# A transformer layer on one core: the head's values by single row tiles, the tail's second half turned earlier, kept pairs copied at once

## The chip, the cores and the metric

The kernel runs on one core of a Trainium2 chip. The metric is the device time of one execution in microseconds. The engines are named as the profile names them: PE does the matmuls (PEld is its loading of the stationary operand), ACT the activation functions, DVE the elementwise work and the reductions, POOL small extra work, and SP issues the transfers. Every engine has its own queue and works through it in order; engines wait for one another by semaphores.

## The reference, cut to what matters

One layer of a transformer on 2048 rows of width 1024, in bf16. The attention has 32 heads of width 32, the FFN 3584 units:

```python
def _A_ref(x, wqkv, wo):                       # H = 32, Dh = 32
    q, k, v = split_heads(x @ wqkv)
    p = softmax(einsum("bhqd,bhkd->bhqk", q, k) * Dh ** -0.5)
    return merge_heads(einsum("bhqk,bhkd->bhqd", p, v)) @ wo

def _B_ref(x, w1, b1, w2, b2):
    return gelu_tanh(x @ w1 + b1) @ w2 + b2

h = x + _A_ref(layernorm(x), wqkv, wo)
out = h + _B_ref(layernorm(h), w1, b1, w2, b2)
```

## The kernel before, in words

The 2048 rows are 16 row tiles of 128, or four chunks of 512. The 32 heads are eight groups of four. A planner in Python (`Plan`) writes out every engine's instruction list: each operation has a cost in ns, the planner keeps the time at which each engine is free and each buffer ready, and places operations by these times. The hardware then runs the fixed lists, with the waits that the planner derived from buffers read and written.

**The head** (lines 757 to 968) is placed by a list scheduler. A job is a step of one engine: `S` the statistics of a row tile (two `bn_stats` and a `bn_aggr` on DVE, L482 and L484), `R` and `I` the root and the reciprocal for a pair of tiles (POOL L495 to L497, DVE L498), `N` the normalising (DVE L801 or ACT L804), `T` the turning by PE (eight transposes, L512) and `C` its copy into `xnT` (ACT or DVE, L829); row tiles 6 to 13 are turned by DMA (L733). `K` and `Q` are matmuls for the first key group and the first four query groups (L843), `KE`, `QE` their copies (DVE L849, ACT L851), `KS`, `QS` the squares (ACT L859 or DVE). `Kn1` to `Kn4` and `Qn1` to `Qn4` reduce the squares to the largest norm (L870, L876, L877, L881, L886). `V` makes the values of two row tiles for the first two head groups (16 matmuls into one PSUM bank, L898), and `VE` copies them (L910).

A job may start when the jobs it depends on are placed. For each job the scheduler takes the engine on which it ends first, with a surcharge `LEAN` (ns) for DVE; on each engine it takes, among the jobs that can start within `WAIT` ns of the first, the one with the smallest priority number, and of the engines' picks it places the one that starts first. `SP` holds the shifts of the priorities: with the numbers before, `N` of tile tt has tt + 1, `C` tt - 2, `KE` and the like -6 on their own number, and `VE` 100 - 90. The loop ends when both norms are there; values not made by then are made later, by `proj_v` in the list `v_left`.

From the norms comes a bound on the scores, and from it a bias per group (`bias_of`, L708 to L714) that keeps the exponential in range, and a flag: where the bound is small the exponential runs without a bias. The first exponential waits for the first group's bias and flag.

**The middle** runs the attention, 1024 exponentials on ACT (L1215, 128x1024 each), 16 for an item of one head group and 256 rows. PE makes scores (L1206) and weighted values (L1291), and in between it is given steps of a "fill" (L530, the helper `wide`): first the values left over, then the other groups' keys, values and queries, then for each chunk the output projection, the norm and the FFN of the chunk before. The fill has PSUM bank 7 for itself. Near the end the fill makes "early slices" for the last chunk: pairs of FFN units for its first 256 rows, with weights `w_e`, as long as there is time and at most ten pairs (`FC // 2 - AHEAD`). Their sums with the bias (L1786) are kept in `gT_t` until the tail, and the gelu is applied there, since the function table then changes from exponential to gelu.

**The tail** (`tail`) projects the last 256 rows, normalises them (`last_norm(1)`), and runs four more pairs for the first half of the chunk (`for hf in range(2)`, hf 0, `AHEAD` is 4), then turns the second half (`last_turn(1)`: 16 transposes L512, two DVE copies L1439), then the same four pairs for the second half, then the other pairs, then the second FFN matmul and the output. `gelu` (L1827) reads each pair from PSUM, `held_gelu` (L1847) applies the function to four kept units at a time.

Of the kernel before, what the change touches and what calls it, by code (L numbers as in the profile page):

```python
# [13 lines left out]
P = 128  # L14
# [221 lines left out]
def build_kernel(nc, A_x, A_wqkv, A_wo, B_w1, B_b1, B_w2, B_b2, out):  # L236
# [120 lines left out]
    lnf, B_lnf0 = sb("lnf", [P, NLN, 4, 2], dt.float32, nbufs(1))  # L357
    half, (B_half,) = sb("half", [P, 4], dt.float32)
    lnd, B_lnd = sb("lnd", [P, NLN, 4], dt.bfloat16, nbufs(NLN * 2))
    lnb, B_lnb = sb("lnb", [P, 8, 2], dt.float32, nbufs(8))  # L360
# [4 lines left out]
    pool(lambda g: g.memset(lnf[:], 0.0), writes=B_lnf0 + B_lnm + B_lnv)  # L365
    pool(lambda g: g.memset(half[:], 0.5), writes=[B_half])
    warm, (B_warm,) = sb("warm", [P, 1], dt.float32)
    rcp, B_rcp = sb("rcp", [P, 2, 8], dt.float32, nbufs(2))
# [336 lines left out]
    def bias_of(g, tc):  # L705
        i = tc * 2 + g // 4
        b = biasm[:, g, tc:tc + 1]
        dve(lambda v: v.tensor_tensor(b, qmax[:, i, g % 4:g % 4 + 1], kmax[:, g:g + 1], ALU.add),  # L708
            reads=[B_qmax[i], B_kmax[g]], writes=[B_bias[g][tc]])
# [4 lines left out]
        dve(lambda v: v.tensor_scalar(b, b, -0.505 * SCALE, None, ALU.mult), reads=[B_bias[g][tc]], writes=[B_bias[g][tc]])  # L714

# [175 lines left out]
    def vals_job(p):  # L891
        tt = 2 * p

        def emit(eng, bank):
            for u in range(2):
                tc, o = (tt + u) // 4, ((tt + u) % 4) * P
                for dc in range(DC):
                    pe(lambda p, u=u, tc=tc, o=o, dc=dc: p.matmul(ps[:, bank, u * 256:(u + 1) * 256], xnT[tc][:, dc, o:o + P], wv[:, dc, 0:256],  # L898
                                                                  start=(dc == 0), stop=(dc == DC - 1)),
                       reads=B_wv[0:1] + [B_xnTf[tt + u]], writes=[B_ps[bank]] if dc in (0, DC - 1) else [], inc=(dc == DC - 1), cost=mm(256))  # L900
        job(("V", p), {E.PE: 1790}, [("C", tt), ("C", tt + 1)], 100 + p, B_wv[0:1] + B_xnTf[tt:tt + 2], [], emit, opens=True)

        def emit2(eng, bank):
            o_ap = V[:, tt:tt + 2, 0:256]
            i_ap = ps[:, bank, :].rearrange("p (u c) -> p u c", u=2)
            B_o = [B_V[tt][0], B_V[tt + 1][0]]
            if eng == E.DVE:
                dve(lambda v: v.tensor_copy(o_ap, i_ap), reads=[B_ps[bank]], writes=B_o, cost=700)
            else:
                act(lambda a: a.activation(o_ap, i_ap, ACT.Copy), reads=[B_ps[bank]], writes=B_o, cost=510)  # L910
# [22 lines left out]
    while ("kn", 0) not in marks or ("qn", 0, 0) not in marks:  # L933
        cand = {}
        for j in jobs.values():
# [23 lines left out]
        j.emit(e_, bank)  # L959
        if j.bank:  # L960
            held.discard(bank)
# [798 lines left out]
    def early_slices():  # L1760
# [7 lines left out]
        while early["n"] < FC // 2 - AHEAD and not early["stop"]:  # L1768
# [7 lines left out]
            for u in range(2):  # L1776
                for dc in range(DC):
                    B = B_w1_[k * 4 + dc // 2:k * 4 + dc // 2 + 1]
                    if dc % 4 == 0 and coming:
# [3 lines left out]
                         [B_ps[bank]] if dc in (0, DC - 1) else [], dc == DC - 1, quad)  # L1783
            for u in range(2):
                fc = 2 * bk + u
                dve(lambda v, fc=fc, u=u: v.tensor_tensor(gT[:, fc, 0:256], ps[:, bank, u * 256:u * 256 + 256], b1f[:, fc:fc + 1].to_broadcast([P, 256]), ALU.add),  # L1786
                    reads=[B_ps[bank], Bf_b1f], writes=[B_gT[2 * fc]], cost=420)
        while coming:
            coming.popleft()()

    def tail():
# [318 lines left out]
```

## Time and profile before

| | |
|---|---|
| median of 3 runs | 1130.21 us (1129.67 to 1131.08) |
| profiled execution | 1129.03 us |
| its span | 1127.2 us |
| first exponential | 48.45 us |
| end of the last exponential, start of the tail | 1030.65 us |
| busy over the span | PE 95%, ACT 92%, DVE 60%, weight loads 58% |

The span is the time from the first to the last instruction that the profile holds; the execution's own time has 1.8 us more around it. Times in the rows are microseconds from the start of the span. In the timeline a row is start, length, engine, line, operation, result<-operands, shapes, count; what stands in brackets is the idle time of that engine just before it and what ended it. In the list of waits a row is the waiting instruction, what it waited for, microseconds in total, number of times, the longest. In groups of one line the three numbers behind the count are the shortest, the median and the longest duration in ns.

### The profile page before, as it was taken

Reading aid. Unit: us, or ns where it says so; the run is one execution under the profiler, and the core shown is the slowest. Engines: PE = TensorE matmul, PEld = TensorE weight load, DVE = VectorE, ACT = ScalarE, POOL = GpSimd, SP = SyncE. Lnnn points to the kernel's source line nnn. Section 1 sums busy time; section 2 is a strip of 40 time slices with the busy share of each in tenths; the row PEclk is TensorE's granted clock in tenths of the full one; section 3 lists DMA queues with packets and bytes.
Section 4 is the critical chain, followed back from the end, with each engine's and each line's share of the span. In section 5 each row is a group of like instructions: output and inputs, shape, how many; then the busy total and the mean of one; then the engine's idle time right before and its main releaser. Section 6 shows DMA issues by size and latency. Waiting matters only on the chain.

```text
span 1127.2 us, 55337 instructions
## 1 busy us (share of the span) xinstructions
PE 1074.9 (95%) x25677; PEld 653.2 (58%) x25682; DVE 681.2 (60%) x1241; ACT 1032.3 (92%) x1149; POOL 21.7 (2%) x67
## 2 busy tenths in 40 slices
PE   6999999998999999999999999999999999999999
PEld 3556465644444446765444457775444676675888
DVE  7565656555767786555678785455577856556021
ACT  6799999999999999999999999999999999996510
POOL 2100000000000000000000000000000000000000
PEclk9999999999999999999999999999999999999999
DMA  9701000023422343424513432402224531427763
GB/s 273 130 22 41 22 3 12 14 63 77 93 68 77 107 114 97 126 77 97 86 59 88 127 115 79 124 23 74 77 80 124 149 83 49 117 83 197 183 160 90
DMA packets 212792, 103.72 MB, mean 92 GB/s; under 512 B 62032, under 2 KB 209488, under 8 KB 212560
## 3 DMA queue, kind: packets, MB, share of 16 engines
q1 hardware_dynamic: 212560, 100.18, 34.0%
q8 instruction: 201, 3.29, 1.2%
q14 instruction: 31, 0.25, 0.1%
HBM read 91.23 MB, written 4.19 MB: 85 GB/s over the span
## 4 chain that ended last, share of the span: by engine, by line
ACT 43%; PE 42%; issue 9%; DVE 5%; DMA 0%; SPq 0%; ACTq 0%; DVEq 0%
ACT PT L1215 40%; PE ps L530 18%; PE ps L525 8%; PE ps L1291 7%; PE ps L1206 6%; ACT tm L1610 2%; PE ps L843 1%; PE ps L898 1%; DVE Rg L1304 1%; DVE Rg L1302 1%; DVE QT L1306 1%; PE ps L637 0%; DVE gT L1594 0%; DVE lnst L482 0%; DVE rcp L1303 0%
## 5 line engine op out<-in xcount | busy, mean ns | idle before, releaser
L1215 ACT ACTIVATE PT<-ps 128x1024 bf16<-128x1024 f32 x1024 | 951.9, 1163 | 4.6 <-DVE biasm L714 2.6
L1240 DVE TENSOR_TENSOR FS<-PT 128x1024 bf16<-128x1024 bf16 x256 | 174.9, 688 | 140.7 <-ACT PT L1215 118.4
L1291 PE MATMUL ps<-PT,V 128*32 128x256 bf16 x4096 | 223.3, 274 | 9.2 <-DVE QT L1306 4.7
L1206 PE MATMUL ps<-QT,KT 32*128 32x256 bf16 x4096 | 203.9, 273 | 19.3 <-ACT PT L1215 13.9
L530 PE MATMUL ps<-hnT,w 128*32 128x512 bf16 (+1 forms) x2880 | 174.0, 367 | 4.3 <-DVE gT L1594 2.7
L530 PE MATMUL ps<-w,gT 128*32 128x256 bf16 x5376 | 173.2, 273 | 0.8 <-issue 0.6
L1206 PEld LDWEIGHTS ps<-QT,KT 32*128 32x128 bf16 x4096 | 60.9, 92 | 170.5 <-ACT PT L1215 148.4
L530 PEld LDWEIGHTS ps<-w,gT 128*32 128x32 bf16 x5376 | 141.0, 97 | 10.8 <-issue 4.6
L1291 PEld LDWEIGHTS ps<-PT,V 128*32 128x32 bf16 x4096 | 105.2, 96 | 55.1 <-issue 13.8
L1291 PE MATMUL ps<-PT,ones 128*32 128x256 bf16 x2048 | 129.2, 273 | 0.0
L530 PEld LDWEIGHTS ps<-hnT,w 128*32 128x32 bf16 x2880 | 65.7, 96 | 71.2 <-issue 27.1
L1594 DVE TENSOR_TENSOR gT<-ps,b1f 128x512 bf16<-128x512 f32 x84 | 57.9, 690 | 51.3 <-PE ps L530 50.9
L1291 PE MATMUL ps<-FS,ones 128*32 128x256 bf16 x1024 | 73.4, 277 | 0.0
L1291 PEld LDWEIGHTS ps<-PT,ones 128*32 128x32 bf16 x2048 | 55.0, 97 | 10.7
L530 PE MATMUL ps<-xnTe,wk 128*32 128x512 bf16 x832 | 56.5, 381 | 0.5 <-DVE KT L585 0.5
L1611 DVE SCALAR_TENSOR_TENSOR gT<-tm,gT 128x1024 bf16<-128x1024 bf16 x42 | 51.1, 1219 | 3.4 <-ACT tm L1610 2.9
L1609 DVE SCALAR_TENSOR_TENSOR tm<-tm,gT 128x1024 bf16<-128x1024 bf16 x42 | 51.3, 1221 | 0.8
L1610 ACT ACTIVATE tm<-tm 128x1024 bf16<-128x1024 bf16 x42 | 50.9, 1215 | 0.0
L525 PE MATMUL ps<-w,gT_t 128*128 128x256 bf16 x448 | 49.1, 273 | 0.0
L525 PEld LDWEIGHTS ps<-w,gT_t 128*128 128x128 bf16 x448 | 43.8, 98 | 5.1
L1291 PEld LDWEIGHTS ps<-FS,ones 128*32 128x32 bf16 x1024 | 26.9, 95 | 24.2 <-issue 20.9
L1827 ACT ACTIVATE gT_t<-ps,b1f 128x256 bf16<-128x256 f32 (+1 forms) x36 | 15.6, 482 | 24.7 <-PE ps L525 24.7
(142 smaller groups left out, 893.9 us busy)
## 6 DMA issues: line engine op xcount, KB each, us to landing
w<-in_B_w_dram SPq DMA_DIRECT2D x45, 512.0 KB, 3.9
w<-in_B_w_dram SPq DMA_DIRECT2D x168, 128.0 KB, 3.7
w_t<-in_B_w_dram SPq DMA_DIRECT2D x12, 512.0 KB, 6.1
w_e<-in_B_w_dram SPq DMA_DIRECT2D x44, 128.0 KB, 2.4
xr<-in_A_x_dram SPq DMA_DIRECT2D x16, 256.0 KB, 6.9
wk<-in_A_wqkv_dram SPq DMA_DIRECT2D x16, 256.0 KB, 3.2
wq<-in_A_wqkv_dram SPq DMA_DIRECT2D x16, 256.0 KB, 5.2
w<-in_B_w_dram SPq DMA_DIRECT2D x14, 256.0 KB, 6.1
```

The costliest lines, as they stand in the source:

```text
L525: pe(lambda p: p.matmul(ps[:, bank, lo:lo + n], lhsT, rhs, start=start, stop=stop), reads=reads, writes=writes, inc=inc, cost=mm(n))
L530: pe(lambda p, r=r: p.matmul(ps[32 * r:32 * r + 32, bank, lo:lo + n], lhsT[:, 32 * r:32 * r + 32], rhs, start=start, stop=stop, tile_posit ...
L843: pe(lambda p, dc=dc: p.matmul(ps[:, bank, :], w_of(dc), xnT[tc][:, dc, :], start=(dc == 0), stop=(dc == DC - 1)), reads=B_w + xn_of(tc), ...
L1206: pe(lambda p, k=k, kt=kt, r=r, b=b: p.matmul(ps[:, b, k * 256:(k + 1) * 256], KT[32 * r:32 * r + 32, g, kt * P:(kt + 1) * P], QT[32 * r:3 ...
L1215: act(lambda a, safe, i=i, b=b: a.activation(PT[:, o_, 2 * i:2 * i + 2, :], ps[:, b:b + 2, :], ACT.Exp, bias=0.0 if safe else biasm[:, g, ...
L1240: dve(lambda v: v.tensor_tensor(FS[:, f_, :, :], PT[:, o_, :, 0:256], PT[:, o_, :, 256:512], ALU.add), reads=B_PT[o_], writes=[B_FS[f_]], ...
L1291: pe(lambda p, d=d, r=r, lhsT=lhsT, rhs=rhs, n=n: p.matmul(ps[32 * r:32 * r + 32, OD, d * 256:(d + 1) * 256], lhsT, rhs, start=(start and ...
L1594: dve(lambda v: v.tensor_tensor(gT_[0][:, fcs[0]:fcs[0] + k, lo:lo + n], ps[:, bank, :].rearrange("p (u c) -> p u c", u=k), b1f[:, fcs[0]: ...
L1609: (E.DVE, lambda v: v.scalar_tensor_tensor(t_, t_, GB, x_, ALU.add, ALU.mult), [Bt] + Bx, [Bt], 1220),
L1610: (E.Activation, lambda a: a.activation(t_, t_, ACT.Tanh, scale=GK), [Bt], [Bt], 946),
L1611: (E.DVE, lambda v: v.scalar_tensor_tensor(x_, t_, 1.0, x_, ALU.add, ALU.mult), [Bt] + Bx, Bx, 1220)])
L1827: act(lambda a: a.activation(gT[:, fc, lo:lo + n], ps[:, bank, o:o + n], ACT.Gelu_apprx_tanh, bias=b1f[:, fc:fc + 1], scale=1.0), reads=[B ...
```

## The change

Head: `bias_of` takes the sum of the norms and the maximum with the bound in one operation (`safe_c` holds the bound per partition), and the shift and the scale in another, three operations in place of four. `WAIT` goes from 500 to 50 ns, the surcharges `LEAN` and the priority shifts `SP` get other numbers, and the surcharges hold only while statistics are still to be placed, except for `VE` and `QS`. A pair of values is made by two jobs, `V` for the first row tile and `W` for the second (priority 99), in the same bank. Values left over are copied by DVE in place of ACT.

Tail: the second half is turned before the fourth pair of the first half instead of behind it. Early slices: one addition for the two units of a pair, in place of two.

```diff
+    safe_c, (B_safe,) = sb("safe_c", [P, 1], dt.float32)
...
+    pool(lambda g: g.memset(safe_c[:], SAFE / (0.505 * SCALE)), writes=[B_safe])
...
-        dve(lambda v: v.tensor_tensor(b, qmax[:, i, g % 4:g % 4 + 1], kmax[:, g:g + 1], ALU.add),
-            reads=[B_qmax[i], B_kmax[g]], writes=[B_bias[g][tc]])
+        dve(lambda v: v.tensor_scalar(b, qmax[:, i, g % 4:g % 4 + 1], kmax[:, g:g + 1], safe_c[:, 0:1], ALU.add, ALU.max),
+            reads=[B_qmax[i], B_kmax[g], B_safe], writes=[B_bias[g][tc]])
...
-        dve(shift_op(b, b), reads=[B_bias[g][tc]], writes=[B_bias[g][tc]])
-        dve(lambda v: v.tensor_scalar(b, b, -0.505 * SCALE, None, ALU.mult), reads=[B_bias[g][tc]], writes=[B_bias[g][tc]])
+        dve(lambda v: v.tensor_scalar(b, b, -SAFE / (0.505 * SCALE), -0.505 * SCALE, ALU.add, ALU.mult), reads=[B_bias[g][tc]], writes=[B_bias[g][tc]])
...
-    WAIT = 500.0
-    LEAN = {"N": 600.0, "C": 1000.0, "M": 600.0, "KE": 300.0, "QE": 300.0, "QS": 5000.0, "VE": 5000.0}
+    WAIT = 50.0
+    LEAN = {'N': 1000, 'C': 600, 'M': 1000, 'KE': 300, 'KS': 0, 'QE': 5000, 'QS': 300, 'VE': 600}
...
-        def emit(eng, bank):
-            for u in range(2):
-                tc, o = (tt + u) // 4, ((tt + u) % 4) * P
+        def half(u):
+            tc, o = (tt + u) // 4, ((tt + u) % 4) * P
+
+            def emit(eng, bank):
                 for dc in range(DC):
...
+            return emit
+        job(("V", p), {E.PE: 895}, [("C", tt), ("C", tt + 1)], 100 + p, B_wv[0:1] + B_xnTf[tt:tt + 2], [], half(0), opens=True)
+        job(("W", p), {E.PE: 895}, [("V", p)], 99, B_wv[0:1] + B_xnTf[tt + 1:tt + 2], [], half(1), bank=("V", p))
...
-        job(("VE", p), {E.DVE: 700, E.Activation: 510}, [("V", p)], 100 + SP[5], [], [], emit2, bank=("V", p))
-
-    SP = (1.0, 0.0, 1.0, -2.0, -6.0, -90.0)
+        job(("VE", p), {E.DVE: 700, E.Activation: 510}, [("W", p)], 100 + SP[5], [], [], emit2, bank=("V", p))
+
+    SP = (1.0, 0.0, 2, 1, 3, -90)
...
-            end, st, e_ = min(o, key=lambda q: q[0] + (LEAN.get(j.name[0], 0.0) if q[2] == E.DVE else 0.0))
+            lean = LEAN.get(j.name[0], 0.0) if any(("S", tt) in jobs for tt in range(NT)) or j.name[0] in ("VE", "QS") else 0.0
+            end, st, e_ = min(o, key=lambda q: q[0] + (lean if q[2] == E.DVE else 0.0))
...
-        if j.bank:
+        if j.bank and j.name[0] != "W":
             held.discard(bank)
...
         if ("V", p) not in jobs and ("VE", p) in jobs:
+            if ("W", p) in jobs:
+                jobs[("W", p)].emit(E.PE, bank_of[("V", p)])
             jobs[("VE", p)].emit(E.Activation, bank_of[("V", p)])
-    v_left = [proj_v(2 * p, 0, "act") for p in range(NT // 2) if ("V", p) in jobs]
+    v_left = [proj_v(2 * p, 0) for p in range(NT // 2) if ("V", p) in jobs]
...
-            for u in range(2):
-                fc = 2 * bk + u
-                dve(lambda v, fc=fc, u=u: v.tensor_tensor(gT[:, fc, 0:256], ps[:, bank, u * 256:u * 256 + 256], b1f[:, fc:fc + 1].to_broadcast([P, 256]), ALU.add),
-                    reads=[B_ps[bank], Bf_b1f], writes=[B_gT[2 * fc]], cost=420)
+            fc = 2 * bk
+            dve(lambda v, fc=fc: v.tensor_tensor(gT[:, fc:fc + 2, 0:256], ps[:, bank, :].rearrange("p (u c) -> p u c", u=2),
+                                                 b1f[:, fc:fc + 2].unsqueeze(2).to_broadcast([P, 2, 256]), ALU.add),
+                reads=[B_ps[bank], Bf_b1f], writes=[B_gT[2 * fc], B_gT[2 * fc + 2]], cost=690)
...
             for bk in range(n, n + AHEAD):
+                if hf == 0 and bk == n + AHEAD - 1:
+                    yield from last_turn(1)
                 bank = fbanks.next()
...
-            if hf == 0:
-                yield from last_turn(1)
```

More of the change, by code (lines that the diff above doesn't have):

```diff
@@ L892, in vals_job @@
         tt = 2 * p
-        def emit(eng, bank):
-            for u in range(2):
-                tc, o = (tt + u) // 4, ((tt + u) % 4) * P
+        def half(u):
+            tc, o = (tt + u) // 4, ((tt + u) % 4) * P
+            def emit(eng, bank):
                 for dc in range(DC):
-                    pe(lambda p, u=u, tc=tc, o=o, dc=dc: p.matmul(ps[:, bank, u * 256:(u + 1) * 256], xnT[tc][:, dc, o:o + P], wv[:, dc, 0:256],
-                                                                  start=(dc == 0), stop=(dc == DC - 1)),
+                    pe(lambda p, dc=dc: p.matmul(ps[:, bank, u * 256:(u + 1) * 256], xnT[tc][:, dc, o:o + P], wv[:, dc, 0:256],
+                                                 start=(dc == 0), stop=(dc == DC - 1)),
                        reads=B_wv[0:1] + [B_xnTf[tt + u]], writes=[B_ps[bank]] if dc in (0, DC - 1) else [], inc=(dc == DC - 1), cost=mm(256))
-        job(("V", p), {E.PE: 1790}, [("C", tt), ("C", tt + 1)], 100 + p, B_wv[0:1] + B_xnTf[tt:tt + 2], [], emit, opens=True)
+            return emit
+        job(("V", p), {E.PE: 895}, [("C", tt), ("C", tt + 1)], 100 + p, B_wv[0:1] + B_xnTf[tt:tt + 2], [], half(0), opens=True)
+        job(("W", p), {E.PE: 895}, [("V", p)], 99, B_wv[0:1] + B_xnTf[tt + 1:tt + 2], [], half(1), bank=("V", p))
         def emit2(eng, bank):
```

## The prediction

> **What bounds the kernel now.** I read the page's head, then busy times by stretch, then who waits for whom, then the timeline of the head and of the tail.
>
> ```profile
> span 1127.2 us, 55337 instructions
> PE 1074.9 (95%) x25677; PEld 653.2 (58%) x25682; DVE 681.2 (60%) x1241; ACT 1032.3 (92%) x1149; POOL 21.7 (2%) x67
> ...
> 48.45:1030.65 982.20, 946.30 (x24508) 549.87 (x24500) 627.26 (x1126) 980.10 (x1067) 8.65 (x21) 1.00 0.30 79
> 1030.65:1124.70 94.05, 92.77 (x879) 79.30 (x880) 20.27 (x34) 21.30 (x43) 1.14 (x3) 1.00 0.63 164
> 9.00:46.92 37.92, 34.33 (x266) 23.34 (x274) 26.86 (x60) 29.20 (x38) 9.59 (x29) 1.00 0.95 215
> ...
> ACT PT L1215 <- DVE biasm L714: 2.6, 1, 2.6
> ACT PT L1215 <- PE ps L1206: 1.9, 4, 1.1
> ```
>
> The columns of the three stretches are length, then busy PE, PEld, DVE, ACT, POOL, the granted clock (1.00 everywhere), DMA share, GB/s. There are three stages. The head, up to the first exponential at 48.45, has PE busy 34.33 of the 37.92 us between the first transpose and the last norm matmul. In the middle ACT is busy 980.10 of 982.20 us. Its length is fixed by 1024 exponentials and 42 tanh, and in all of it the exponentials wait for PE only 1.9 us. The tail is PE's, 92.77 of 94.05 us.
>
> PE never runs out of work for long in the middle: what the exponentials leave of it goes to projections and FFN, and what is not done by 1030.65 is done in the tail. So a step taken out of the head counts as far as PE no longer idles there. Work merely pushed behind the first exponential comes back, in the middle or in the tail.
>
> **Head, the last row tiles.** The critical stretch of the head runs from the statistics of the last row tile to the first exponential.
>
> ```profile
> 16.22 1.89 PE L843 MATMUL ps<-xnTe,wk 128*128 128x512 bf16 x7 [1.67 <-ACT xnTe L829]
> 25.94 0.69 DVE L849 CAST QT<-ps 128x512 bf16<-128x512 f32 x1 [1.50 <-PE ps L843]
> ...
> 34.05 1.41 DVE L482 BATCH_NORM_STATS2 lnst<-xr 128x6 f32<-128x512 bf16 x2
> 37.37 0.55 DVE L801 TENSOR_SCALAR xr<-xr,lnf,rstd 128x1024 bf16<-128x1024 bf16 x1
> 38.03 1.23 ACT L804 ACTIVATE xr<-xr,lnb,rstd 128x1024 bf16<-128x1024 bf16 x1
> 39.31 0.62 PE L512 MATMUL ps<-ident,xr 128*128 128x128 bf16 x8 [0.29 <-ACT xr L804]
> 39.63 1.93 ACT L829 ACTIVATE xnTl<-ps 128x1024 bf16<-128x1024 bf16 x2
> 41.84 1.67 PE L843 MATMUL ps<-xnTl,wk 128*128 128x512 bf16 x7
> 43.35 1.91 PE L898 MATMUL ps<-wv,xnTl 128*128 128x256 bf16 x16
> 44.18 0.63 ACT L859 ACTIVATE sqk<-KT 128x512 bf16<-128x512 bf16 x1
> 45.19 0.40 PE L870 MATMUL ps<-sqk,blk 128*32 128x512 bf16 x4
> 46.68 0.23 PE L881 MATMUL ps<-dg,ones_pp 128*128 128x128 bf16 x1 [1.09 <-DVE dg L877]
> 47.27 0.16 DVE L708 TENSOR_TENSOR biasm<-qmax,kmax 128x1 f32<-128x1 f32 x1
> 47.66 0.15 DVE L703 TENSOR_SCALAR biasm<-biasm 128x1 f32<-128x1 f32 x1
> 47.85 0.15 DVE L714 TENSOR_SCALAR biasm<-biasm 128x1 f32<-128x1 f32 x1
> 48.45 13.86 ACT L1215 ACTIVATE PT<-ps 128x1024 bf16<-128x1024 f32 x15 [2.56 <-DVE biasm L714]
> ...
> L910 ACT ACTIVATE V<-ps x8: 575/597/605, 16.0 to 45.3; 128x512 bf16<-128x512 f32 x8
> ```
>
> Tile 14 is normalised on DVE (37.37), tile 15 on ACT until 39.26, and both transposed copies go through ACT one after the other, to 41.56, before the last key matmuls at 41.84. The change drops the surcharge on DVE once no statistics are left.
> - Tile 15 on DVE behind tile 14: 37.37 + 2 x 0.55 = 38.47 in place of 39.26, so 0.79 earlier. Copies on two engines: the second no longer waits for the first, so one of two halves of 1.93 (0.96) goes, less about 0.2 for the later of two transposes. The last key group could start about 1.5 us earlier.
> - Before that, DVE loses 1.50 us waiting for a query copy (25.94) and 0.69 us in making it. With the window at 50 in place of 500 ns and queries at 5000, neither should happen. But smaller surcharges for transposed copies (600 for 1000), value copies (600 for 5000) and query squares (300, none stood there) may put other work on DVE ahead of the last statistics. Between all 2.19 us won and as much lost again by four ops of 0.55, I take 0.7 won.
> - Biases: four ops from 47.27 to 47.85 (three shown, the flag lies between) become three, the shift of L703 being folded in. The step between two starts is 0.58 / 3 = 0.19, so 0.19 earlier; it happens eight times, but only the first is waited for in the rows above.
> - The norm matmuls (45.19) stood behind a pair of value matmuls, while the squares ended at 44.81. Half a pair holds PE for half as long: about 0.2 earlier.
>
> So the first exponential could come 1.5 + 0.7 + 0.19 + 0.2 = 2.6 us earlier. PE cannot give all of that. All eight value pairs (L910, x8) are made in the head, 1.91 us of PE each by the row at 43.35. What PE saves is idle time:
> - 0.29 ahead of the transposes at 39.31: gone.
> - 1.09 ahead of the matmul at 46.68, while DVE reduces the key norm: a half of 8 value matmuls is 0.95, and it fits, since values are then still left over. I take 0.9.
> - 1.67 at 16.22, where the first keys wait for copies of tiles 2 and 3: the split lets transposes in between two halves, but ACT still makes those copies. From nothing to all of it; I take 0.3.
>
> Head: 0.29 + 0.9 + 0.3 = 1.5 us. Of the 2.6 us the other 1.1 is value work not yet done when the exponentials start, about half a pair to a pair. Bounds: nothing (the halves don't fit, copies move to DVE) to 0.29 + 1.09 + 1.67 = 3.05.
>
> Where the spilled work is paid for also shows:
>
> ```profile
> L1215 ACT ACTIVATE PT<-ps 128x1024 bf16<-128x1024 f32 x1024 | 951.9, 1163 | 4.6 <-DVE biasm L714 2.6
> 254.12 0.15 DVE L714 TENSOR_SCALAR biasm<-biasm 128x1 f32<-128x1 f32 x1
> 259.51 41.48 ACT L1215 ACTIVATE PT<-ps 128x1024 bf16<-128x1024 f32 x45 [1.13 <-PE ps L1206]
> 80.00:110.00 30.00, 29.76 (x876) 19.86 (x871) 17.05 (x37) 29.80 (x33) 0.00 (x0) 1.00 0.12 39
> ```
>
> The bias of the last key group lands at 254.27. The 45 exponentials of the next row stand (41.48 - 1.16) / 44 = 0.916 us apart, so exponential 225, the first of that group (14 items of 16 before it), is due at 48.45 + 224 x 0.916 = 253.7, or later by the few tenths waited before. So the first phase already runs without slack on PE, 29.76 of 30 us in the stretch shown, and exponentials that start earlier than PE's work allows would wait there.
>
> One removed cost is nothing: left-over values copied by DVE in place of ACT, since all eight copies are in the head now. The extra memset on POOL (about 0.1 us by its neighbours) is covered by the wait for the first rows; without that cover it costs 0.1.
>
> **Tail.**
>
> ```profile
> 1043.07 1.00 DVE L1427 TENSOR_SCALAR x_t<-hch_t,lnf,rstd 128x1024 bf16<-128x1024 bf16 x2
> 1043.91 3.66 PE L525 MATMUL ps<-hn_t,w_t 128*128 128x256 bf16 x32
> 1047.40 1.06 PE L512 MATMUL ps<-ident,x_t 128*128 128x128 bf16 x16
> 1048.05 1.29 DVE L1439 COPY hn_t<-ps 128x1024 bf16<-128x1024 bf16 x2 [3.97 <-PE ps L512]
> 1049.39 3.67 PE L525 MATMUL ps<-hn_t,w_e 128*128 128x256 bf16 x32 [0.94 <-DVE hn_t L1439]
> ...
> L1786 DVE TENSOR_TENSOR gT_t<-ps,b1f x18: 406/415/426, 1003.8 to 1040.9; 128x256 bf16<-128x256 f32 x18
> L1594 DVE TENSOR_TENSOR gT<-ps,b1f 128x512 bf16<-128x512 f32 x84 | 57.9, 690 | 51.3 <-PE ps L530 50.9
> ```
>
> Pairs three and four of the first half are the 32 matmuls at 1043.91, then come 16 transposes, then PE waits 0.94 for their copies. With the transposes after the third pair they start at 1043.91 + 3.66 / 2 = 1045.7. Their input is there at 1044.07, so they don't wait, with 1.6 us to spare. The copies start 0.65 behind and end at 1047.7; pair four runs from 1046.8 to 1048.6. The wait goes: 0.94. If the cover is short, it is the copy that comes late, at most 0.94 again. ACT's gelus of the fourth pair come 1.06 later and it idles behind them (no wait of PE for ACT stands in these rows). Bounds 0.6 to 0.94; I take 0.94. The moved step issues no DMA and passes no other instruction on DVE's queue; the weight loads that follow it on SP wait for their pairs, as before.
>
> Kept pairs: two additions of 0.415 become one of 128x512, by its twin L1594 0.69. That is 0.14 less DVE time for each of nine pairs, off the path; at most it returns fill bank 7 earlier. I take 0.1, between 0 and 0.6.
>
> **Sum.** 1.5 + 0.94 + 0.1 = 2.5, against the profiled execution of 1129.03 us (span 1127.2): 1126.5. That execution lies 1.18 below the median of 1130.21, so the forecast for the median is 1127.7, 0.22% faster. About 0.2%, 2.26 us, is what a measurement can tell here, so this is close to the edge.
>
> **The rivals.**
> *B, ACT alone is the bound.* PE has gaps in the middle (982.20 - 946.30 = 36 us), and left-over values disappear in them. Then the whole 2.6 us of the head count: 2.6 + 0.94 + 0.1 = 3.6, so 1126.6; with the start gap at 16.22 gone too, 5. For it: weight loads fill only 549.87 of 982.20 us. Against it: the deadline at 254 us. [...]
>
> *C, the head stays as it is.* More copies on DVE hold up the statistics, or copies of left-over values stand on ACT (0.60 each) ahead of the first exponential. Only the tail remains: 1130.21 - 1.0 = 1129.2, no measurable change.
>
> *D, slower.* Values come last on PE and in halves, so several pairs are left when the norms are done. In the middle they have a single fill bank and wait for their DVE copies (0.69 for 128x512), so each costs 1.91 + 0.69 = 2.6. With the exponentials 2.6 earlier and the tail 1.0 better, the sign turns above 3.6 / 2.6 = 1.4 pairs left; with three, 7.8 - 3.6 = 4.2 us slower, 1134.4. For it: the two numbers given to values, 99 and 100, are the largest on PE. Against it: PE is nearly gapless from 16 us, so three pairs can be left only if it idles some 4 us more than now.
>
> *E, no split after all.* Halves run back to back because nothing else is ready; then 0.9 of the head goes, giving 1128.6.
>
> **How the numbers follow.** A (my sum) 0.40, own range 1126.6 to 1128.8; B 0.20; C 0.16; E 0.10; D 0.14. A lies on the edge and gives 0.28 to faster and 0.12 to same; B is faster; C and E are same with 0.22 of their 0.26, the rest faster by a larger early gap; D is slower with 0.13 and same with 0.01. Faster 0.52, same 0.35, slower 0.13. The range goes from B with all gaps gone, 1125, to just past C and one more wait of 1.13 as at 259.51 for two key groups, 1131.5.
>
> **What would show it.** The first exponential near 46; no PE wait behind the key norm's reduction; the last two copies on different engines; the last transposes between pairs three and four and no wait at the second half; 1 to 2 value pairs through the fill helper after the first exponential. Wrong would be: exponentials waiting for PE by more than 4 us in all, statistics ending after 35.7, or a ninth early pair missing.

## The result, and the profile after

The changed kernel takes 1126.4 us (median; 1125.15 to 1127.55), the kernel before 1129.67 us beside it. The ratio is 0.9969, with a 95% interval of 0.9957 to 0.9980: 3.5 us less, between 2.3 and 4.9. Run once more beside other kernels it came to 0.9970 (0.9958 to 0.9982). The forecast was 2.5 us less. The profiled execution of the changed kernel takes 1126.72 us, 2.31 less than that of before.

Its span is 1124.9 us. Its busy times by stretch are these (first exponential to last, then to the end, then first transpose to first scores; the columns are those of the prediction):

```profile
47.69:1029.45 981.76, 946.38 (x24512) 550.87 (x24505) 626.48 (x1111) 980.22 (x1066) 8.69 (x21) 1.00 0.29 79
1029.45:1124.90 95.45, 92.60 (x879) 79.33 (x880) 20.47 (x34) 21.32 (x43) 1.15 (x3) 1.00 0.55 162
9.94:47.24 37.30, 36.02 (x279) 24.27 (x282) 25.85 (x61) 29.31 (x38) 9.80 (x29) 1.00 0.84 224
```

Before, the last exponential ended at 1030.65 of a span of 1127.2, so its tail was 96.55. By stages the 2.3 us of the two spans are: first exponential 0.76 earlier (48.45 to 47.69), middle 0.44 shorter (982.20 to 981.76), tail 1.10 shorter (96.55 to 95.45). The head's 0.76 is less than the 1.5 forecast. Why, the timeline of the head says (rows of PE, its weight loads, DVE and ACT, in order of time):

```profile
29.67 0.21 DVE L486 BATCH_NORM_AGGREGATE lnmv<-lnst 128x2 f32<-128x12 f32 x1
33.16 1.23 ACT L805 ACTIVATE xr<-xr,lnb,rstd 128x1024 bf16<-128x1024 bf16 x1
34.73 1.89 PE L844 MATMUL ps<-xnTl,wk 128*128 128x512 bf16 x8
36.46 1.06 PE L514 MATMUL ps<-ident,xr 128*128 128x128 bf16 x16
37.10 1.29 DVE L828 COPY xnTl<-ps 128x1024 bf16<-128x1024 bf16 x2 [3.30 <-PE ps L514]
38.87 1.67 PE L844 MATMUL ps<-xnTl,wk 128*128 128x512 bf16 x7
40.44 1.91 PE L900 MATMUL ps<-wv,xnTl 128*128 128x256 bf16 x16
42.28 0.40 PE L871 MATMUL ps<-sqk,blk 128*32 128x512 bf16 x4
42.61 1.92 PE L900 MATMUL ps<-wv,xnTl 128*128 128x256 bf16 x16
44.37 0.22 PE L882 MATMUL ps<-dg,ones_pp 128*128 128x128 bf16 x1
44.43 1.91 PE L900 MATMUL ps<-wv,xnTl 128*128 128x256 bf16 x16
45.45 0.15 DVE L715 TENSOR_SCALAR biasm<-biasm 128x1 f32<-128x1 f32 x1
46.37 0.60 ACT L914 ACTIVATE V<-ps 128x512 bf16<-128x512 f32 x1 [1.21 <-PE ps L900]
47.24 0.12 PEld L1213 LDWEIGHTS ps<-QT,KT 32*128 32x128 bf16 x8 [0.42 <-ACT V L914]
47.69 1.02 ACT L1222 ACTIVATE PT<-ps 128x1024 bf16<-128x1024 f32 x1 [0.72 <-PE ps L1213]
```

The last statistics end at 29.88 (before 35.7), the last normalisation at 34.39. The last transposes then stand on PE behind the third key group and begin at 36.46 (before 39.31). Both last copies are on DVE, which had been idle for 3.3 us, at 0.65 each. The last key group starts at 38.87, 2.97 earlier than the 41.84 of before, and the bias is done at 45.60, 2.40 earlier than 48.00. No wait stands at the norm matmul (44.37): the value matmuls at 42.61 lie over the reduction. But three groups of 16 value matmuls follow the last key group, where before there was one. The last of them hold a PSUM bank until ACT has copied it (46.37 + 0.60 = 46.97), the scores at 47.24 wait for that copy, and the exponential waits 0.72 for the scores, no longer for the bias.

The other part of the head's shortfall is at its start. The first rows of PE, of the changed kernel and then two of before:

```profile
9.94 2.16 PE L514 MATMUL ps<-ident,xr 128*128 128x128 bf16 x16 [9.94 <-ACT xr L805]
12.18 3.51 PE L900 MATMUL ps<-wv,xnTe 128*128 128x256 bf16 x16
15.53 1.95 PE L514 MATMUL ps<-ident,xr 128*128 128x128 bf16 x32
18.47 1.67 PE L844 MATMUL ps<-xnTe,wk 128*128 128x512 bf16 x7 [0.99 <-ACT xnTe L830]
```

```profile
9.04 2.05 PE L512 MATMUL ps<-ident,xr 128*128 128x128 bf16 x16 [9.04 <-DVE xr L801]
11.27 2.38 PE L898 MATMUL ps<-wv,xnTe 128*128 128x256 bf16 x16 [0.18 <-ACT xnTe L829]
```

The first 16 value matmuls took 3.51 us. In the profile of before the same 16 took 2.38, and later ones take 1.91. The stretches above print a granted clock of 1.00 throughout, but that figure hides a slow start, as the last section shows. The experiments show that this length changes from execution to execution (3.51 and 3.27 us in two profiles of the changed kernel), so the two profiles are not equal in it by 1.13 us.

The timeline of the tail of the changed kernel (PE's rows and the copies):

```profile
1042.71 1.91 PE L527 MATMUL ps<-hn_t,w_t 128*128 128x256 bf16 x16
1044.46 1.06 PE L514 MATMUL ps<-ident,x_t 128*128 128x128 bf16 x16
1045.11 1.29 DVE L1446 COPY hn_t<-ps 128x1024 bf16<-128x1024 bf16 x2 [2.29 <-PE ps L514]
1045.35 1.91 PE L527 MATMUL ps<-hn_t,w_t 128*128 128x256 bf16 x16
1047.10 3.66 PE L527 MATMUL ps<-hn_t,w_e 128*128 128x256 bf16 x32
```

The transposes stand between the third and the fourth pair, and the second half (1047.10) follows without a wait: the 0.94 of before is gone. The waits of the exponentials for PE (us in total, times, longest), and the additions of the kept pairs:

```profile
ACT PT L1222 <- PE ps L1213: 2.1, 6, 0.7
```

```profile
L1792 DVE TENSOR_TENSOR gT_t<-ps,b1f x9: 674/683/691, 1002.6 to 1039.4; 128x512 bf16<-128x512 f32 x9
```

Nine early pairs are kept, as before.

### The profile page after: what moved, and what is told of

Read it like the earlier page. It is cut to its first block, busy times and chain, and to the rows that moved or that the text cites. A ratio compares the mean times of both kernels' runs of the same rounds, so it can differ in the third digit from the quotient of the medians.

```text
span 1124.9 us, 55331 instructions
## 1 busy us (share of the span) xinstructions
PE 1075.5 (96%) x25678; PEld 654.7 (58%) x25682; DVE 679.3 (60%) x1223; ACT 1033.6 (92%) x1150; POOL 22.0 (2%) x68
## 4 chain that ended last, share of the span: by engine, by line
ACT 44%; PE 42%; issue 9%; DVE 5%; DMA 0%; ACTq 0%; POOL 0%; DVEq 0%
ACT PT L1222 41%; PE ps L532 18%; PE ps L527 8%; PE ps L1298 7%; PE ps L1213 6%; ACT tm L1617 3%; PE ps L900 1%; PE ps L844 1%; DVE Rg L1311 1%; DVE Rg L1309 1%; DVE QT L1313 1%; DVE gT L1601 0%; DVE lnst L484 0%; DVE rcp L1310 0%; PE ps L639 0%
```

## The experiments

Four theories stand against each other. **P**: PE's time is conserved. A gain of the head counts as far as PE idles less in it, and work moved out of the head comes back later. **S**: the start of the first exponential counts by itself. **B** is the prediction's rival B, ACT alone is the bound. **D** is its rival D, left-over pairs of values cost more than their matmuls.

**The parts alone.** The changed head with the old tail; the earlier turning alone; the merged additions alone.

```
head_only = after, with
-                if hf == 0 and bk == n + AHEAD - 1:
-                    yield from last_turn(1)
...
+            if hf == 0:
+                yield from last_turn(1)
...  and the kept pair added by two operations of 128x256
turn_only = before, with
+                if hf == 0 and bk == n + AHEAD - 1:
+                    yield from last_turn(1)
...
-            if hf == 0:
-                yield from last_turn(1)
slice_only = before, with
-            for u in range(2):
-                fc = 2 * bk + u
...
+            fc = 2 * bk
+            dve(lambda v, fc=fc: v.tensor_tensor(gT[:, fc:fc + 2, 0:256], ps[:, bank, :].rearrange("p (u c) -> p u c", u=2),
...
```

> The changed head alone; tail and early slices as before. Theory P (PE's account: only PE idle time removed counts): the changed kernel has 35.86 - 36.47 and 48.45 - 47.69, that is 1.37 us less PE idle before the first exponential, so 1.4 us less time than before (ratio 0.9988), of it 0.76 as an earlier first exponential and the rest as less waiting later. Theory S (the start of the exponentials counts): 0.8 us less (0.9993). First exponential at 47.7 in both; the second half of the last chunk waits 0.9 us for its turned rows, as before.

> The earlier turning of the second half alone. The 0.94 us wait of PE at the first matmuls of the second half goes and nothing takes its place: 0.9 us less than before (ratio 0.9992), head unchanged with the first exponential at 48.4. Rival (the wait moves, for example to a late gelu): no difference, and a new PE wait of about 0.9 us appears in the tail.

> The kernel before, with the two additions of a kept pair merged into one and nothing else changed. The prediction's term: 0.1 us less (0 to 0.6), so a ratio of 0.9999, between 0.9995 and 1.0000. In the profile nine additions of 128x512 at about 0.69 us instead of 18 of 0.415; nine early pairs as before. Rival: the parts left a rest of 1.3 us against the whole (3.5 against 2.2), and it is this edit that holds it: ratio 0.9988.

The head alone: 1127.55 us, ratio 0.9985 (0.9976 to 0.9994). The turning alone: 1128.66, 0.9996 (0.9987 to 1.0005). The additions alone: 1129.38, 1.0003 (0.9994 to 1.0012). So the head holds about 1.7 us, the turning about 0.5 by its time, and the additions nothing that can be measured. For the head, P's 1.4 us and S's 0.8 both lie within the interval (0.7 to 2.7), so this run does not choose between them. The profile of the turning alone is clearer than its time; PE's rows around the second half:

```profile
1046.18 1.06 PE L512 MATMUL ps<-ident,x_t 128*128 128x128 bf16 x16
1047.08 1.91 PE L525 MATMUL ps<-hn_t,w_t 128*128 128x256 bf16 x16
1048.82 3.44 PE L525 MATMUL ps<-hn_t,w_e 128*128 128x256 bf16 x30
```

The wait is gone, and the tail is 95.52 us (1126.7 - 1031.18), 1.03 less than before; with spans of one decimal this can't be told from the 1.10 of the whole change. With the additions alone the tail is 96.58 (1127.5 - 1030.92) and stays as it was.

**The whole change again**, beside two of the others.

> The changed kernel itself, run again beside the two others. If each timed comparison stands for the kernel and not for the batch, the ratio is 0.9969 within its interval of 0.9957 to 0.9980. If the parts simply add (head 1.7 us, earlier turning 0.45 us), it comes out at 0.9981. In the profile: second FFN matmuls of the tail 2.3 us earlier than before, no wait at the second half; PE stalls that have no shown cause may appear or be missing, as they did in other runs.

1126.29 us against 1129.16, ratio 0.9970: the whole stands. The parts by their times sum to 0.9985 - 0.0004 + 0.0003 = 0.9984 only. Each interval is about 1 us to either side, so the rest of some 1.6 us may be nothing. By plain medians there is no rest: against the kernel before beside them (1129.81, 1129.81 and 1129.16) the parts are 2.26 and 1.15 less and 0.22 more, 3.2 less in all, and the whole is 3.3 less. Its profile has the span 1123.8, first exponential 47.47, tail 95.44.

**The split alone, the new numbers without it, and the whole change without it.**

```
split_only = before, with
-        job(("V", p), {E.PE: 1790}, [("C", tt), ("C", tt + 1)], 100 + p, ...
+        job(("V", p), {E.PE: 895}, [("C", tt), ("C", tt + 1)], 100 + p, ...
+        job(("W", p), {E.PE: 895}, [("V", p)], 99, ...
params_only = after, with values in pairs again, and tail and kept pairs as before
nosplit = after, with values in pairs again
```

> The kernel before, with values made by two jobs of one row tile each, and nothing else. In the order that the planner writes, the last value matmuls still stand ahead of the key norm's matmuls, so the 1.09 us gap behind them stays. Theory P: no change beyond 0.3 us (ratio 1.000). The prediction's step (halves fill the gap) would give 0.9 us less (0.9992) from the split alone.

> The changed head with values in pairs as before; tail and early slices as before. The last key group starts about 3 us earlier because the statistics end near 30 instead of 35.7, and two pairs of values fall behind it and into the wait for the key norm. Theory P: the 1.09 us gap is filled without the split too, 1.0 to 1.5 us less than before (ratio 0.9988), like the whole changed head. If the split is what gains, no more than 0.3 us less (0.9997).

> The changed kernel with values made in pairs again; the new costs, order numbers, three-op bias, earlier turning and merged additions stay. Prediction's step (halves are what fills the wait for the key norm's reduction, 0.9 us): 1127.3 us, ratio 0.9977. Theory P (the wait is filled by whole pairs too, as with the new costs alone, so PE idles as little in the head): the same as the changed kernel, 0.9970, although the last key matmuls start some 0.7 us later behind a whole pair. Theory S (the start of the first exponential counts by itself): 0.7 us longer, 0.9976. Sum of the parts without the split (0.9992, 0.9996 and 1.0003): 0.9991.

Split alone: 1130.87 us, ratio 1.0014 (1.0005 to 1.0023). New numbers alone: 1128.57, 0.9992 (0.9983 to 1.0001). Whole change without the split: 1127.44, 0.9977 (0.9968 to 0.9986). In the split alone the wait at the norm matmul stays as it was:

```profile
44.62 1.91 PE L899 MATMUL ps<-wv,xnTl 128*128 128x256 bf16 x16
46.46 0.40 PE L870 MATMUL ps<-sqk,blk 128*32 128x512 bf16 x4
47.95 0.23 PE L881 MATMUL ps<-dg,ones_pp 128*128 128x128 bf16 x1 [1.09 <-DVE dg L877]
```

Without the split but with all the rest it is gone:

```profile
40.55 1.67 PE L844 MATMUL ps<-xnTl,wk 128*128 128x512 bf16 x7
...
42.12 1.91 PE L899 MATMUL ps<-wv,xnTl 128*128 128x256 bf16 x16
43.96 0.40 PE L871 MATMUL ps<-sqk,blk 128*32 128x512 bf16 x4
44.29 1.92 PE L899 MATMUL ps<-wv,xnTl 128*128 128x256 bf16 x16
46.05 0.22 PE L882 MATMUL ps<-dg,ones_pp 128*128 128x128 bf16 x1
```

What fills the wait is not a half pair but a second pair of values still to be made behind the last key group, and that is there because this group comes earlier against the values (the new costs and order numbers), not because of the split. PE idles 11.23 us ahead of the first exponential here, 11.22 with the split. The split does bring the last key group forward, 40.55 to 38.87, but the first exponential only from 47.92 to 47.69. By time it is worth 0.9 us by the two ratios (0.9977 and 0.9969), which their intervals can't tell from nothing. So the time alone would also fit the 0.9 that the prediction gave to the halves; what speaks against the halves as the filler is the matmul at 46.05, which stands there without a wait.

**Fewer values in the head.** The last pair, and then the last two pairs, are kept back until the head is over and go to the fill helper.

```
left1: -        job(("V", p), {E.PE: 895}, [("C", tt), ("C", tt + 1)], 100 + p, ...
       +        job(("V", p), {E.PE: 895}, [("C", tt), ("C", tt + 1)] + ([("V", p)] if p >= 7 else []), 100 + p, ...
left2: the same with p >= 6
```

> The changed kernel, with the last pair of values (row tiles 14 and 15) kept out of the head and left to the fill. The first exponential comes about 1.5 us earlier than in the changed kernel (46.1 to 46.3), since the bias is ready at 45.6 and the first scores no longer wait for a bank that this pair holds. Theory P: the pair's 1.9 us of PE come back in the middle or the tail, total within 0.4 us of the changed kernel (ratio to before 0.997). Theory S, which is also rival B of the prediction (ACT alone bounds): 1.5 us less than the changed kernel (0.9956).

> The changed kernel with the last two pairs of values kept out of the head and given to the fill. Theory P (PE time is conserved): the 16 value matmuls that fill the wait for the key norm's reduction are gone, the wait of about 1.1 us opens again, so the total is some 0.9 us longer than that of the changed kernel (ratio about 0.998), with fewer early pairs and a longer tail, although the first exponential may come a further 0.5 to 1.9 us earlier. Theory B (only ACT counts): the earlier first exponential is kept to the end, ratio 0.996 or lower. Theory D (single fill bank): each pair left costs 0.7 us besides its matmuls, ratio 0.9985 or more.

One pair kept back: 1126.06 us, 0.9974 (0.9963 to 0.9985), the same as the changed kernel. Two pairs: 1131.83, 1.0024 (1.0014 to 1.0033), slower than before. The stages of one pair kept back, and the additions of its early pairs:

```profile
46.03:1027.13 981.10, 947.38 (x24368) 546.87 (x24360) 625.69 (x1109) 980.30 (x1066) 9.21 (x21) 1.00 0.29 78
1027.13:1124.30 97.17, 94.51 (x896) 80.91 (x896) 20.47 (x34) 21.35 (x42) 1.15 (x3) 1.00 0.54 159
```

```profile
L1792 DVE TENSOR_TENSOR gT_t<-ps,b1f x8: 674/684/692, 1002.2 to 1037.1; 128x512 bf16<-128x512 f32 x8
```

The first exponential comes 1.66 us earlier than in the changed kernel's first profile (1.44 than in its second), the last ends 2.32 earlier (1.23), and nothing of it reaches the end: only eight pairs are early, and the tail is 1.72 longer (97.17 against 95.45). This is as theory P says, and against B and S, whose 0.9956 lies just outside the interval: here an exponential stage that starts and ends earlier is worth nothing, with the same work for PE. Two limits: the fill makes half of the pair (32 matmuls at 44.30) still ahead of the first exponential, and the kernel with bank 6 below loses its ninth early pair too, with no pair moved. So the lost pair by itself does not show that the moved work was paid there; the unchanged time has to carry the argument. With two pairs kept back, the timeline (PE and ACT) and the middle stage:

```profile
43.11 0.23 PE L882 MATMUL ps<-dg,ones_pp 128*128 128x128 bf16 x1 [1.09 <-DVE dg L878]
...
196.76 1.02 ACT L1222 ACTIVATE PT<-ps 128x1024 bf16<-128x1024 f32 x1 [3.95 <-PE ps L1213]
```

```profile
44.99:1032.38 987.39, 951.12 (x24428) 549.47 (x24420) 626.06 (x1110) 980.87 (x1067) 9.11 (x21) 1.00 0.28 77
```

The wait of 1.09 is back, as P expects, because no values are left to fill it. But the kernel is 5.5 us slower than the changed one, where P expected 0.9. The middle has grown by 5.6 us (987.39 against 981.76): the exponentials start 2.7 us earlier, and at 196.76 ACT waits 3.95 us for the scores of a key group whose projections, norms and bias are only just done (the bias between 195.81 and 196.45). This is a key group's deadline, of the kind that the prediction saw at 254 us, hit earlier. D's size and its turning point (between one pair and two) fit better than P's 0.9, but not D's place: 3.95 of the 5.6 us are paid in one wait at 196.76, not pair by pair at the fill bank. Another 0.70 is waited at 279.68, in a stretch at half clock that the profiles of the changed kernel lack (last section).

**The last pair in a bank that the scores don't use.**

```
bank6 = after, with
-            bank = best_bank() if j.opens else ...
+            bank = (None if 6 in held else 6) if j.name == ("V", 7) else best_bank() if j.opens else ...
...  and the copy of that pair asked of DVE
```

> The changed kernel, with the last pair of values in PSUM bank 6 and copied by DVE, so that the first scores don't wait for that copy on ACT. The first scores follow the values at once and the first exponential comes at 46.7 in place of 47.7. PE does the same work in nearly the same time, only the 16 fill matmuls now come behind the first scores. Theory P: 0 to 0.3 us less than the changed kernel. Theory S: 0.9 us less (ratio to before 0.9962).

1128.41 us, 0.9991 (0.9982 to 1.0000): 2.0 us slower than the changed kernel, which neither theory said. PE and ACT at the end of the head:

```profile
46.68 0.40 PE L1213 MATMUL ps<-QT,KT 32*128 32x256 bf16 x8
...
46.78 0.60 ACT L914 ACTIVATE V<-ps 128x512 bf16<-128x512 f32 x1 [1.21 <-PE ps L900]
47.59 1.94 ACT L1222 ACTIVATE PT<-ps 128x1024 bf16<-128x1024 f32 x2 [0.21 <-issue]
```

The scores come without the wait for the bank (46.68), but the copy, emitted by the loop that follows the head, was still made on ACT, and there it stands ahead of the exponential: 0.1 us won. So S is not put to the test. The written order of the middle changed too, with eight early pairs, a tail of 97.19 and a middle of 983.02 us. So a shift of a microsecond in the head can cost an early pair through the order alone.

**Matmuls ahead of the head**, to take the slow first matmuls away: 24 matmuls of ones on PE ahead of the first transposes, in the changed kernel and in the one before. They add work whose result is not used.

```
+    for i_ in range(24):
+        pe(lambda p: p.matmul(ps[:, 7, :], ones_pp[:], ones_pp[:].unsqueeze(1).to_broadcast([P, 4, P]), start=True, stop=True),
+           reads=[B_ones], writes=[B_ps[7]], inc=i_ == 23, cost=mm(512))
```

> The changed kernel with 24 matmuls of no use on PE between 2 and 9 us, where PE has nothing else. The first 16 value matmuls took 3.51 us in the changed kernel's profile and 2.38 in the kernel before, against 1.9 for the later ones, which would be the slow clock of an engine that was idle. If that costs time (theory P): these 16 take 1.9 us, and the whole is 1.0 to 1.5 us less than the changed kernel (ratio to before 0.996). If the head's start is bound by statistics and copies: the 16 are faster, but the first exponential comes no earlier and the total stays (0.997).

> The same 24 matmuls in the kernel before. Its first 16 value matmuls took 2.38 us, so 0.5 us could be won there by theory P (ratio 0.9996), less than in the changed kernel, whose first transposes come 0.9 us later; nothing by the other theory (1.000).

The changed kernel with them: 1128.83 us, 0.9998 (0.9989 to 1.0007). The one before with them: 1130.36, 1.0013 (1.0004 to 1.0022). PE of the first:

```profile
12.03 1.91 PE L903 MATMUL ps<-wv,xnTe 128*128 128x256 bf16 x16 [0.38 <-ACT xnTe L833]
...
38.82 1.67 PE L847 MATMUL ps<-xnTl,wk 128*128 128x512 bf16 x7 [1.23 <-issue]
...
812.55 0.62 PE L535 MATMUL ps<-hnT,w 128*32 128x512 bf16 x8 [1.75 <-issue]
```

The 16 value matmuls take 1.91 us, so the slow start is gone: in both kernels the 16 take 1.91 behind other matmuls, and without them 2.38 to 3.57 by execution; the last section shows the clock behind it. Why the length differs between executions, no run shows. Yet nothing is won. Both kernels are slower than without these matmuls, by 2.4 us (1128.83 against 1126.4) and by 1.1 (1130.36 against 1129.27 beside it). In the changed kernel the gain is there up to the last 8 value matmuls ahead of the last key group (36.54 us in place of 37.77); then PE stops for 1.23 us at that group and for 1.75 in the middle, and no wait explains either. With these matmuls in both, the change is worth 1.5 us (1130.36 to 1128.83), not 3.5.

**What the profiles say when the slow start is taken out.** Each profile is one execution, and the length of the first 16 value matmuls is its draw. In the four kernels with the old head the first exponential follows it one to one, within 0.25:

| kernel | first 16 value matmuls, us | first exponential, us | difference, us |
|---|---|---|---|
| old head: before | 2.38 | 48.45 | 46.07 |
| old head: turn_only | 2.57 | 48.59 | 46.02 |
| old head: slice_only | 3.35 | 49.19 | 45.84 |
| old head: warm_before | 1.91 | 47.80 | 45.89 |
| new head: after | 3.51 | 47.69 | 44.18 |
| new head: after_again | 3.27 | 47.47 | 44.20 |
| new head: head_only | 2.58 | 46.70 | 44.12 |
| new head without split: nosplit | 3.42 | 47.92 | 44.50 |
| new head without split: params_only | 3.20 | 47.53 | 44.33 |
| old head with split: split_only | 2.70 | 49.71 | 47.01 |
| new head: warm_after (waits 1.23 at the last key group) | 1.91 | 47.63 | 45.72 |

At the same slow start the new head is 46.0 - 44.2 = 1.8 us earlier, and the pair of profiles hid 1.1 of it. The last row is the exception: there the stop of 1.23 us takes back what the start had won, and the first exponentials of the two kernels with matmuls ahead are only 0.17 apart (47.80 and 47.63). The split alone makes the old head about 1 us later, as its time says too. With 1.0 to 1.1 of the tail the new head gives 2.8 us, a ratio of 0.9975, inside the measured interval (0.9957 to 0.9980). The remaining 0.7 us to the middle of that interval is not settled.

## Why the prediction was right or wrong

**The time** (1127.7 forecast, 1126.4 measured) and the sign were right. The forecast of 2.5 us less was 1 us short of the measured 3.5; the sum's two large terms held, several reasons behind them did not. The measured time lies in the range given, and 0.2 below the sum's own range of 1126.6 to 1128.8.

**Head, 1.5 us: the size was nearly right, by way of PE's idle time, and in part by luck.** PE idles 12.59 us ahead of the first exponential before and 11.22 after, 1.37 less; the first exponential, at an equal slow start, is 1.8 earlier. The three terms brought 0.29 + 1.09 + 0.68 = 2.06 for the 1.5, and a cost that was not in the sum took 0.90 back; the other 0.21 lies in small gaps. By the terms:
- 0.29 ahead of the last transposes: gone, as said.
- 0.9 of the wait at the key norm: the whole 1.09 went, but the step "a half of 8 value matmuls fits" was wrong as a reason. The split alone leaves the wait at 1.09, whole pairs fill it without the split, and only when no values are left does it return (1.09 with two pairs kept back).
- 0.3 of the 1.67 ahead of the first keys: 0.68 went (0.99 at 18.47).
- Not forecast: the first tile is now normalised on ACT, behind its POOL operands, and PE starts at 9.94 in place of 9.04. That costs 0.90. With the new numbers alone it is the same (9.80, on ACT). The step that failed is the reading of the surcharges: the higher one for normalising on DVE (1000 for 600) was not followed, neither to the first tile nor to the statistics below. That it is this number among the new ones was not tried singly.

**The four sources of "2.6 us earlier".** Statistics: 0.7 taken, 5.8 measured. The prediction set work that DVE might gain against the 2.19 of the query copy; DVE lost work instead. Before, it normalised eight row tiles ahead of the last statistics, after, two; that is six times about 0.5 us. With the new numbers alone it is the same (two tiles, statistics done at 29.73). It brought 2.97 at the last key group and no more, because PE's own order (transposes behind the third key group) then set it. Copies: they went to one engine, DVE, not to two, and were quicker so, 0.65 each for ACT's 0.96. Biases: the three operations end 0.64 after their start, the four ended 0.73 after it, so 0.09 and not 0.19, and no longer on the path. Norm matmuls: the wait behind a value pair stayed: the squares are done at 41.84, the matmuls start at 42.28, so 0.44 against the 0.38 of before.

**"About half a pair to a pair of values not yet done": wrong.** All eight pairs are made in the head. The surplus shows as PE work behind the last key group instead: three groups of 16 value matmuls there, and an exponential that waits for scores rather than for the bias. That it could not be had was right: keeping that pair back moved the first exponential 1.66 us forward and the end not at all. So "work merely pushed behind the first exponential comes back" fits the one pair tried; the tail holds 1.72 of it.

**The deadline.** It was placed at 254 us; in the changed kernel the wait there is 0.44 (at 258.11), against 1.13 before at 259.51. The profile of before has a PE stop of 0.76 without a shown cause at 259.1, so its wait was no clean sign of a deadline. That such a deadline can bind is shown by the two pairs kept back, at 196.76.

**Tail, 0.94: right.** The wait went, and the tail shortened by 1.0 to 1.1, in the whole and alone. **Kept pairs, 0.1:** nothing measurable, and 0.683 us in place of 2 x 0.415 as worked out.

**The rivals.** B's time (1126.6) is closer to the measured one than the sum's, but its mechanism is contradicted by the pair kept back: by it, the 1.2 to 2.3 us by which the exponentials end earlier would have reached the end. The weight loads, which spoke for B, fill 56% of the middle here (550.87 of 981.76 us); that did not mean that PE had room, for the pair kept back gained nothing (0.9974 against 0.9969). C is refuted by the head alone (0.9985). D did not happen, and two pairs kept back show that it could have: its turning point of 1.4 pairs fits, but by luck, since the price is paid at a deadline and not at the fill bank. E's premise, that without halves the wait stays, is false; its time cannot be told from the sum's. Of the five signs that were to show the sum right, two came: no wait of PE behind the key norm's reduction, and the last transposes between pairs three and four with no wait behind them. Three did not: the first exponential came at 47.69 and not near 46, the last two copies are on one engine, and no pair goes to the fill. Of the signs named in advance as wrong, none came: the exponentials wait 2.1 us for PE in all, the statistics end before 35.7, and nine early pairs are there.

## What to carry to other kernels

Where one engine is busy nearly all the time, count how much less it idles up to the end of the stretch, not how much earlier the next stage starts. Then test the count by pushing one unit of work out of the stretch, and a second one: here the first was free and the second cost 5 us at a deadline. When several edits go together, take each away as well as trying each alone: here the edit that looked like the filler was not it. And before two single profiles are subtracted, compare the duration of the same first work in both; here it differed by 1.1 us, half of what the profiles showed as gain. Look at the durations for this, not at the mean clock.

## What was not expected of the hardware

The first 16 value matmuls took 2.38 to 3.57 us by execution, and 1.91 with matmuls ahead of them. The traces show the clock behind it. Eleven of the 14 hold a record of the granted clock; it begins, at full clock, at 12.27 us in before and at 15.50 in the changed kernel, and the views print the empty time ahead of it as 1.00. In before the value matmuls start some 213 ns apart until 12.29 us and 109 ns apart from there; in the changed kernel they stay 213 apart to the last. In the nine profiles where the record begins while these 16 run, they take 1.91 us plus half of the time from their start to the record's, within 0.06.

A mean clock of 0.998, as some executions show it, has a place too. Four profiles (the head alone, the new numbers alone, the split alone, two pairs kept back) have one stretch of 3.41 us at half clock, between 272.9 and 280.4 us. In the head alone (columns as before, the clock third from the end):

```profile
272.88:276.29 3.41, 3.09 (x44) 1.06 (x36) 0.84 (x3) 2.37 (x3) 0.00 (x0) 0.50 0.16 37
```

The next exponential waits 1.29 us for PE there (at 276.54), with the new numbers alone 1.31 (at 277.77). No execution of the changed kernel had such a mean, of 13; with the new numbers alone 9 of 11 had one, with matmuls ahead 8 and 7 of 11, with two pairs kept back 6 of 11. So a part of what these lack may be the clock. Their executions do not settle it: those below 1.00 are 0.9 to 1.4 us longer in five kernels (both with matmuls ahead among them) and not clearly longer in three. Why the clock fell, no run shows: just ahead of the fall PE was busy for 1.56 to 1.81 of 3.42 us in all four, with no idle time longer than 1.44, but the changed kernel has such a stretch too (1.78, from 269.46) and no fall.

PE also stops, within a group of matmuls, for times that differ from profile to profile (0.34 and 1.40 us at the place below) and that no wait explains. One and the same place, the last seven or eight matmuls of a group near 431 us, reads so in the changed kernel and in the one with only the new head:

```profile
430.43 0.40 PE L532 MATMUL ps<-w,gT 128*32 128x256 bf16 x7 [0.34 <-issue]
```

```profile
431.45 0.40 PE L532 MATMUL ps<-w,gT 128*32 128x256 bf16 x7 [1.40 <-issue]
```

Stops of over 0.5 us are missing in the changed kernel, in its second profile, without the split, with the new numbers alone and with one pair kept back (with two as well, but there the deadline sets the middle); in these five the middle takes 981.76, 980.89, 981.43, 982.64 and 981.10 us. They are there (0.85 to 1.97 in sum) in before, head_only, turn_only, slice_only, split_only, bank6 and both kernels with matmuls ahead, whose middle takes 982.20, 983.25, 982.59, 981.73, 983.37, 983.02, 983.53 and 983.80. The means, 981.6 and 982.9, differ by about as much as the stops last (with the three among them that have the stretch at half clock left out, 981.3 and 982.8). This could hold the unsettled 0.7 us, and part of what the parts alone lack; whether a kernel has such stops in every execution, single profiles can't say. What ties the stops together is their place in PE's instruction list. Counted along it, with matmuls, weight loads and semaphore instructions as the traces hold them, all 30 stops of over 0.2 us in the middle that no wait explains, in the 14 profiles, begin at a count that leaves 189 to 194 on division by 256; by chance about one in 43 would. The two of over 0.5 us in before, at 259.08 and 432.06 us (0.76 and 0.58), lie 7424 instructions apart, 29 x 256. The stop of 1.23 us in the head leaves 211 and stays open. What holds PE at these places, no row shows.
